# A band-attention and two-mixture kernel whose second mixture enters the list scheduler's plan, with scores and values of a half block in one piece

## The chip, the cores and the metric

The kernel runs on one core of a Trainium2 chip. Its time is the device time of one launch in microseconds (us). Engines are named as in the profile: PE (TensorE, matmuls and transposes; PEld its weight loads), DVE (VectorE), ACT (ScalarE), POOL (GpSimd) and SP, whose queue issues the loads and stores.

## The reference

Three stages on 2 x 768 tokens of 512 channels (8 heads of 64). The `scores` have a bias by distance, and all but the first `n_global` = 8 keys and the `n_local` = 96 latest are masked.

```python
scores = scale * np.matmul(q, k.transpose(0, 1, 3, 2)) + bias
a = np.exp(np.where(keep, scores, -1e9) - max); a = a / (sum(a) + 1e-9)
x = np.matmul(a, v)                              # heads side by side: B, S, 512
xk, xr = mu * x + (1.0 - mu) * x_prev            # mu_k and mu_r
k = np.maximum(xk @ w_k, 0.0);  v = k * k @ w_v  # 512 -> 1024 -> 512
x = v / (1.0 + np.exp(-(xr @ w_r)))
xn = (x - mu) / np.sqrt(var + 1e-06) * g_ln
out = x + np.maximum(xn @ w_ch1, 0.0) @ w_ch2    # 512 -> 2048 -> 512
```

The weights arrive as 64-bit floats. The accuracy wanted is that of 32-bit floats, so each matmul outside attention is done as three: high part by high part, high by low, low by high.

## The kernel before

**Tiles and stages.** Attention goes through 12 blocks of 128 tokens, each in two half blocks of 4 heads. A half block's chain is: scores on PE (`plan_scores`, L577) into two banks, DVE's minimum (L588), ACT's exponential (L594), PE's transposes (L612), ACT's copy of them (L428), PE's values (L626). Heads of 64 channels use the PE array by halves: scores two row halves, values two column halves, and other matmuls use the whole array. Scores and values are each planned as two operations of two heads. The first mixture has 6 groups of 256 tokens: POOL and DVE mix the input (L747 to L759), PE makes r (L796) and k (L830), ACT and DVE the square of the relu (L839, L840; POOL its low part, L845), PE v (L865 to L867, into the bank pair "b45"), DVE evicts v times r (L876), which frees the tanh's place that ACT needs for the next r (L801). The second mixture has 3 chunks of 512 tokens, each of 16 blocks f of 128 hidden channels: an up of 12 matmuls of 512 columns (L1017), ACT's relu (L1019), DVE's low part (L1020), then downs of 4 x 3 matmuls (L1032 to L1034).

**Weights.** A tile of 128 x 512 weights is loaded as 512 KB of integer pairs (the `stage` buffers and `tp`) and converted: a copy of the high words (ACT, POOL), three bit operations on DVE, the high part on ACT, the low part on DVE or POOL. There are 52 such tiles: 20 for the first mixture, and 32 for the second, of which 6 (EARLY) are in the plan and 26 (LATE) come behind it.

**What sets the order.** `Plan.play` (L134) is a list scheduler: operations with a cost on each engine that can do them, their inputs, the rooms (buffers) that they need and a due time. It takes, again and again, the operation that can start first, by due time where two can. Attention, the first mixture, the first 26 weights and the norms of chunk 0 are in that plan. The second mixture and the other weights are not: `mixture2` (L1041) is written behind it as loops (up f, then down f-1), and the later weights' conversions go, some steps at a time, in between. Their order on an engine's queue is left to the framework's own ordering, which draws conversions ahead into the first mixture's end. Engines run their queues in order.

Of the kernel before, what the change touches and what calls it, by code (L numbers as in the profile page):

```python
# [16 lines left out]
P = 128  # L17
# [16 lines left out]

CLOCK = {"PE": 8.0, "ACT": 8.0, "DVE": 9.5, "POOL": 8.0, "SP": 2.5}
# [4 lines left out]
TP_FROM = 20  # L40
LOW = {"POOL": 1440}


TM = (3, 9)
LNF = 12
# [46 lines left out]
def run(generator):  # L92
    for _ in generator:
        pass


# [8 lines left out]
class Plan:  # L105
# [11 lines left out]
    def op(self, engines, fn, reads=(), writes=(), rooms=(), due=0.0, behind=(), size=0):  # L117
# [13 lines left out]
        self.ops.append((engines, fn, deps, rooms, due, size))  # L131
        return i

    def play(self):  # L134
# [11 lines left out]
        dma = 0.0  # L146
        trace = []
        while open_:
            best = None
            for i in open_:  # L150
                engines, _, _, rooms, due, _ = self.ops[i]
# [21 lines left out]
            engines, fn, _, rooms, _, size = self.ops[i]  # L173
# [7 lines left out]
            end = t + engines[e]  # L181
            self.clock[e] = end
# [21 lines left out]
class Fast:  # L204
# [3 lines left out]
    def __init__(self, ctx, tc, a, w, ident):  # L208
# [4 lines left out]
        self.done = set()  # L213
        self.shut = set()
# [86 lines left out]

# [6 lines left out]

    def w_load(self, src):
        slot = self.slots.pop(0)  # L310
        raw = self.t([P, 512, 2], slot, I32, bufs={"stage": 2, "tp": 3}.get(slot, 1))
        self.nc.sync.dma_start(raw.rearrange("p n w -> p (n w)"), src.bitcast(I32))
        return slot, raw

    def w_split(self, slot, raw, hi, lo, scale):


        nc = self.nc
        low, high = raw[:, :, 0], raw[:, :, 1]
        y = self.t([P, 512], "cv", I32, bufs=2)  # L320
        yf = y.bitcast(F32)


        nc.scalar.activation(yf, high.bitcast(F32), AF.Copy, scale=2.0**-112)
        yield
        nc.vector.tensor_scalar(low, low, 29, None, ALU.logical_shift_right)
        yield
        nc.vector.scalar_tensor_tensor(low, high, -(1 << 31), low, ALU.bitwise_and, ALU.bitwise_or)
        yield
        nc.vector.scalar_tensor_tensor(y, y, 3, low, ALU.logical_shift_left, ALU.bitwise_or)  # L330
        if slot in ("stage", "tp", "nb"):
            self.slots.append(slot)
        yield
# [10 lines left out]
    def w_stream(self, items):  # L344


        self.items, self.raws = items, []
        self.bg = self.w_steps()
# [956 lines left out]
```

## Time and profile before

| what | value |
|---|---|
| time, median of 3 runs | 579.66 us (578.03 to 581.67) |
| profiled execution, own time | 578.45 us |
| its span, first to last instruction | 576.7 us |
| PE busy / DVE / ACT / POOL | 545.0 / 301.5 / 219.7 / 163.8 us |

Times in the rows further on count from the span's start. "Stretches" rows show how long each engine was busy in an interval, and the clock that was granted to PE, 1.00 being full (2.4 GHz). A wait's row names the engine and line that was waited for. The chain is the work that ended last, followed back from the end; a matmul that stands in it has its share of the elapsed time, which is shorter than the busy time of one matmul, since matmuls overlap. From 0 to 10 us the kernel loads and prepares, from 10 to about 152 it does attention, up to about 300 the rest of the first mixture, and up to 568 the second.

### The profile page before, as it was taken

How to read it: one execution, taken by the hardware profiler on the slowest of the kernel's cores; microseconds unless marked ns; L12 is line 12 of the kernel's file. 1: busy time of each engine (PE TensorE's matmuls, PEld its weight loads, DVE VectorE, ACT ScalarE, POOL GpSimd, SP SyncE). 2: the span in 40 equal slices, each digit the busy share in tenths (PEclk: the TensorE clock that was granted, in tenths of full speed). 3: DMA queues.
4: the chain of work that ended last, by engine and by line, in shares of the span. 5: the costliest groups of instructions: out<-in, count | busy, mean ns of one | idle time of the engine just before them, and what ended most of it. 6: DMA issues, size and time to landing. Idle time of an engine off the chain costs nothing.

```text
span 576.7 us, 8113 instructions
## 1 busy us (share of the span) xinstructions
PE 545.0 (95%) x3082; PEld 444.5 (77%) x3082; DVE 301.5 (52%) x651; ACT 219.7 (38%) x478; POOL 163.8 (28%) x202
## 2 busy tenths in 40 slices
PE   5979799999879999999799999999999999999995
PEld 3656577877679888989687888888888887888884
DVE  4877788886887364458959991243010133111012
ACT  3777787776753423235525650121011111101010
POOL 3466577644887535561310000010000000000000
PEclk9899999999999999999999999999999999999999
DMA  9899556332512010006424640001000001000002
GB/s 167 196 201 217 135 145 158 107 107 52 205 47 63 2 36 2 1 0 180 149 64 159 205 122 0 1 0 74 0 2 0 1 1 74 0 1 0 1 0 78
DMA packets 57307, 42.59 MB, mean 74 GB/s; under 512 B 49068, under 2 KB 49068, under 8 KB 57260
## 3 DMA queue, kind: packets, MB, share of 16 engines
q1 hardware_dynamic: 57084, 41.99, 27.3%
q8 instruction: 26, 0.43, 0.3%
q14 instruction: 21, 0.17, 0.1%
q0 software_dynamic: 32, 0.00, 0.0%
q10 hardware_dynamic: 144, 0.00, 0.0%
HBM read 38.84 MB, written 3.15 MB: 73 GB/s over the span
## 4 chain that ended last, share of the span: by engine, by line
PE 79%; DVE 9%; ACT 4%; DMA 3%; issue 1%; POOL 1%; SPq 1%; ACTq 0%; DVEq 0%; POOLq 0%
PE b L1017 23%; PE b L1032 8%; PE b L1034 8%; PE b L1033 8%; PE b L830 6%; PE b L796 6%; PE b L626 4%; PE b L577 3%; PE b L612 3%; PE b L865 2%; PE b L867 2%; PE b L866 2%; PE b L529 2%; ACT m L428 1%; DVE rt L752 1%
## 5 line engine op out<-in xcount | busy, mean ns | idle before, releaser
L1020 DVE SCALAR_TENSOR_TENSOR w<-b,w 128x512 fp32r<-128x512 f32 x48 | 33.1, 690 | 154.2 <-ACT w L1019 154.2
L1019 ACT ACTIVATE w<-b 128x512 fp32r<-128x512 f32 x48 | 28.7, 597 | 171.4 <-PE b L1017 171.3
L1032 PE MATMUL b<-w,w 128*128 128x512 f32 x192 | 75.6, 394 | 0.1
L1034 PE MATMUL b<-w,w 128*128 128x512 f32 x192 | 75.3, 392 | 0.0
L1033 PE MATMUL b<-w,w 128*128 128x512 f32 x192 | 75.0, 391 | 0.0
L986 POOL TENSOR_SCALAR st<-st 128x1 f32<-128x1 f32 x12 | 2.7, 225 | 174.2 <-DVE st L984 174.0
L830 PEld LDWEIGHTS b<-qA,w 128*128 128x128 f32 x384 | 48.1, 191 | 2.5 <-issue 1.2
L830 PE MATMUL b<-qA,w 128*128 128x256 f32 x384 | 48.9, 283 | 0.7 <-DVE rt L840 0.7
L594 ACT ACTIVATE tp<-tp,mn 128x232 f32<-128x232 f32 (+1 forms) x96 | 44.4, 466 | 5.6 <-DVE mn L588 5.4
L845 POOL TENSOR_TENSOR m<-rt,m 128x512 fp32r<-128x512 f32 x21 | 31.1, 1483 | 50.1 <-ACT m L841 50.1
L1032 PEld LDWEIGHTS b<-w,w 128*128 128x128 f32 x192 | 36.0, 188 | 9.0 <-DVE xg L1037 1.1
L1034 PEld LDWEIGHTS b<-w,w 128*128 128x128 f32 x192 | 36.0, 188 | 8.1 <-DVE w L1020 0.3
L1033 PEld LDWEIGHTS b<-w,w 128*128 128x128 f32 x192 | 36.1, 188 | 7.6
L752 DVE SCALAR_TENSOR_TENSOR rt<-xg,vec,rt 128x256 f32<-128x256 f32 x48 | 34.4, 762 | 10.9 <-POOL rt L747 10.9
L588 DVE CUSTOM_DVE_ANT_0 tp<-b,ln 128x232 f32<-128x232 f32 (+1 forms) x96 | 32.2, 372 | 14.2 <-PE b L577 13.9
L1017 PE MATMUL b<-kh,m 128*128 128x512 f32 x128 | 36.5, 394 | 0.0
L865 PE MATMUL b<-w,m 128*128 128x512 f32 x84 | 33.5, 399 | 3.0 <-ACT e L801 3.0
L700 POOL TENSOR_TENSOR w<-cv,w 128x512 fp32r<-128x512 f32 x20 | 27.8, 1392 | 23.0 <-ACT w L693 17.6
L867 PE MATMUL b<-w,m 128*128 128x512 f32 x84 | 33.2, 395 | 0.0
L866 PE MATMUL b<-w,m 128*128 128x512 f32 x84 | 33.1, 394 | 0.0
L612 PE MATMUL b<-ident,tp 128*116 128x128 f32 (+1 forms) x176 | 30.4, 284 | 1.7 <-ACT tp L594 1.5
L747 POOL TENSOR_SCALAR rt<-xg,vec 128x256 f32<-128x256 f32 x48 | 30.1, 641 | 1.7 <-DVE xg L666 0.8
(202 smaller groups left out, 1092.5 us busy)
## 6 DMA issues: line engine op xcount, KB each, us to landing
stage<-in_moe_w_ch_dram SPq DMA_DIRECT2D x22, 512.0 KB
tp<-in_moe_w_ch_dram SPq DMA_DIRECT2D x10, 512.0 KB
stage<-in_moe_w_k_dram SPq DMA_DIRECT2D x8, 512.0 KB
stage<-in_moe_w_v_dram SPq DMA_DIRECT2D x8, 512.0 KB
out_dram<-xg SPq DMA_DIRECT2D x12, 256.0 KB
m<-in_v_dram SPq DMA_DIRECT2D x10, 192.0 KB
qA<-in_q_dram SPq DMA_DIRECT2D x7, 256.0 KB
stage<-in_moe_w_r_dram SPq DMA_DIRECT2D x2, 512.0 KB
```

Of the source, the lines that this page charges most:

```text
L594: nc.scalar.activation(t, t, AF.Exp, bias=mn.tile[:, k : k + 1], scale=-1.0, accum_out=sm.tile[:, h : h + 1])
L612: nc.tensor.transpose(b.tile[0:w, c, k * P : (k + 1) * P], tp.tile[:, k, c * w : (c + 1) * w], self.ident)
L752: nc.vector.scalar_tensor_tensor(y.tile[:, u], z, v, y.tile[:, u], ALU.mult, ALU.add)
L796: nc.tensor.matmul(b.tile, *seq[s], start=s == 0, stop=s == 11)
L830: nc.tensor.matmul(o, l, r, start=s == 0, stop=s == 11)
L865: nc.tensor.matmul(ps, hi, wh, start=f == 0, stop=False)
L866: nc.tensor.matmul(ps, hi, wl, start=False, stop=False)
L867: nc.tensor.matmul(ps, lo, wh, start=False, stop=f == 7)
L1017: nc.tensor.matmul(ps, l, r, start=s == 0, stop=s == 11)
L1032: nc.tensor.matmul(ps, hi[:, sl], wh, start=f == 0, stop=False)
L1033: nc.tensor.matmul(ps, hi[:, sl], wl, start=False, stop=False)
L1034: nc.tensor.matmul(ps, lo[:, sl], wh, start=False, stop=f == 15)
```

## The change

The second mixture is in the plan: `plan_second`, `plan_up` and `plan_down` replace `mixture2`, `m2_up` and `m2_down`, and all 52 weight tiles are converted by `plan_weight`. A late weight's low part may go to DVE or POOL, and the copy of its high words to ACT or POOL. Scores of a half block (now L472) and its values (L522) are one operation each. The planner adds 95 ns to a PE operation that uses the array in another way than the one before (`mode`), and some of its costs differ. The norms of the next chunk stand at blocks 8 to 11 of a chunk instead of 12 to 15, and the small operations that test the tokens outside the band (`last`) are planned too. No arithmetic of the outputs is changed.

```diff
-                if j + 1 < NTOK // 512 and f >= LNF:
-                    self.flush()
-                    run(self.m2_norm(j + 1, f - LNF))
...
-TP_FROM = 20
-LOW = {"POOL": 1440}
-TM = (3, 9)
-LNF = 12
+LATE0, LATE1 = -10.0, 3.3
+TP_FROM, TP_TO = 24, 44
+LOW, LATE_LOW = {"POOL": 1440}, {"DVE": 715, "POOL": 1500}
+LNF = 8
...
+    SWITCH = 95.0
...
             end = t + engines[e]
+            if e == "PE" and way != mode:
+                end += self.SWITCH
+                mode = way
...
-        for j in range(2):
-            c = 2 * hf + j
-            s = hf if n == 0 else 0
-            def scores(e, j=j, c=c):
-                for k in (2 * j, 2 * j + 1):
...
-            p.op({"PE": 40 + 1.6 * w}, scores, reads, [("S", i, j)], banks + [self.Q, self.K], due + 0.5 * j)
+        def scores(e):
+            for k in range(4):
+                r, c = slice((k % 2) * D, (k % 2 + 1) * D), 2 * hf + k // 2
+                nc.tensor.matmul(S(k), self.qT(n)[r, c], self.kT()[r, c, c0:c1], start=True, stop=True)
...
+        p.op({"PE": 3.4 * w}, scores, reads, [("S", i)], banks + [self.Q, self.K], due, mode="rows")
...
-            op = p.op({"PE": 218 * m}, values, [("pT", i), ("v", n % 3)], [("O", n, hf, j)], [self.O[n], self.V[n], y], due + 9 + j)
+        op = p.op({"PE": 436 * m}, values, [("pT", i), ("v", n % 3)], [("O", n, hf)], [self.O[n], self.V[n], y], due + 9, mode="columns")
...
-        p.op({"ACT": 670, "POOL": 1100}, lambda e: self.copy(e, yf(), high().bitcast(F32), 2.0**-112), [R], [C], [raw, cv, w], due - 2, behind=behind)
-        p.op({"DVE": 460}, lambda e: nc.vector.tensor_scalar(low(), low(), 29, None, ALU.logical_shift_right), [R], [(R, 1)], [raw], due - 2)
+        p.op({"ACT": 670, "POOL": 850}, lambda e: self.copy(e, yf(), high().bitcast(F32), 2.0**-112), [R], [C], [raw, cv] + wr, due - 2, behind=behind)
+        p.op({"DVE": 500}, lambda e: nc.vector.tensor_scalar(low(), low(), 29, None, ALU.logical_shift_right), [R], [(R, 1)], [raw], due - 2)
...
-        p.op({"DVE": 745} if scale is not None else LOW, rest, [C, HI], [key], [cv, w], due)
-        return w
+        p.op({"DVE": 745} if scale is not None else (LOW if j < 20 else LATE_LOW), rest, [C, HI], [key], [cv] + wr, due)
...
+            self.plan_second(j, x, at[NG])
+            p.op({"DVE": 3000}, lambda e: last(), due=at[NG] + 150)
             self.trace = p.play()
-            last()
-        self.deep = 2
-        self.slots = ["stage", "stage", "tp"]
-        self.w_stream([getattr(self, f"{k}_item")(*r) for k, *r in LATE])
...
+    def plan_second(self, j0, x, start):
+        nc, a, p = self.nc, self.a, self.plan
+        for i, (k, *r) in enumerate(LATE):
+            due = start + LATE0 + LATE1 * i
+            if k == "w1":
+                self.plan_w1(j0 + i, *r, due, [x[-1]] if r[0] == 2 else [])
...
+        for j in range(n):
+            acc = [self.bank_room(3), Room("b45", 1, self.banks), None, self.bank_room(6)]
+            for f in range(16):
+                at = start + 88 * j + 5.5 * f
+                self.plan_up(j, f, at)
+                self.plan_down(j, f, at + 4, acc)
+                if j + 1 < n and LNF <= f < LNF + 4:
+                    self.plan_norm(j + 1, f - LNF, at, self.loads if j == 0 else [])
...
+    def plan_up(self, j, f, due):
...
+        self.up = [p.op({"PE": 2750}, products, reads, [U], [b] + self.xn_rooms[j], due, behind=self.up)]
+        p.op({"ACT": 600}, lambda e: nc.scalar.activation(u.tile[:, 0], b.tile, AF.Relu), [U], [(U, 0)], [b, u], due + 3)
...
+    def plan_down(self, j, f, due, acc):
...
+            p.op({"PE": 688}, products, [(U, 0), (U, 1), ("w2", f)], [("acc", j, tb)], [u, room], due + 0.1 * tb)
```

Where lines move: scores L577 to L472, transposes L612 to L507, values L626 to L522, k L830 to L747, r L796 to L713, v L865 to L782, its eviction L876 to L793, up L1017 to L915, down L1032 to L938, the relu's low part L1020 to L923; on DVE the conversion's L326, L328, L330, L337, L339 to L591, L592, L593, L599, L601.

The instruction order of PE in attention, where one half block's values and the next one's scores stood in two parts, before:

```order
L626 MATMUL b_290_1567<-m_287_1538,m_216_1143 64x128 x4
L612 MATMUL b_292_1597<-ident,tp_1445 116x128 x8
L577 MATMUL b_295_1612<-kh_139,qA_126 128x232
L577 MATMUL b_296_1613<-kh_139,qA_126 128x232
L529 MATMUL b_297_1617<-ident,kh_139 128x128 x4
L577 MATMUL b_295_1612<-kh_139,qA_126 128x232
L577 MATMUL b_296_1613<-kh_139,qA_126 128x232
```

and at a place of the new order:

```order
L507 MATMUL b_294_1609<-ident,tp_1499 116x128 x2
L472 MATMUL b_295_1613<-kh_139,qA_126 128x232
L472 MATMUL b_296_1614<-kh_139,qA_126 128x232
L472 MATMUL b_295_1613<-kh_139,qA_126 128x232
L472 MATMUL b_296_1614<-kh_139,qA_126 128x232
L426 MATMUL b_298_1624<-ident,kh_139 128x128 x4
L507 MATMUL b_294_1609<-ident,tp_1499 116x128 x6
```

Of 24 half blocks, 9 had their scores split and 5 their values; now none has: four score rows stand together, and the values are "L522 x8".

POOL's order behind attention (rt and qA belong to the first mixture's input, w to a converted weight, m to the square's low part), before:

```order
L759 TENSOR_TENSOR kh_1877<-rt_1876,kh_1877 128x512
L759 TENSOR_TENSOR kh_1877<-rt_1891,kh_1877 128x512
L747 TENSOR_SCALAR rt_1939<-xg_735,vec_121 128x256 x2
L747 TENSOR_SCALAR rt_1961<-xg_735,vec_121 128x256 x2
L759 TENSOR_TENSOR qA_1940<-rt_1939,qA_1940 128x512
L759 TENSOR_TENSOR qA_1940<-rt_1961,qA_1940 128x512
L845 TENSOR_TENSOR m_363_2015<-rt_2014,m_363_2015 128x512
L845 TENSOR_TENSOR m_366_2033<-rt_2032,m_366_2033 128x512
```

and now, where a weight's copy (L329) has come in ahead of qA's two low parts:

```order
L601 TENSOR_TENSOR w_340_1883<-cv_1882,w_340_1883 128x512
L601 TENSOR_TENSOR w_343_1907<-cv_1906,w_343_1907 128x512
L664 TENSOR_SCALAR rt_1964<-xg_782,vec_121 128x256 x2
L664 TENSOR_SCALAR rt_1981<-xg_782,vec_121 128x256 x2
L329 TENSOR_SCALAR cv_2002<-stage_1944 128x512
L676 TENSOR_TENSOR qA_1965<-rt_1964,qA_1965 128x512
L676 TENSOR_TENSOR qA_1965<-rt_1981,qA_1965 128x512
L664 TENSOR_SCALAR rt_2052<-xg_1348,vec_121 128x256 x2
```

DVE's order at the end of the first mixture, where the eviction of a v tile (L876, L793) frees the tanh's place, before:

```order
L337 SCALAR_TENSOR_TENSOR qA_3148<-cv_3166,vec_121,qA_3148 128x512
L337 SCALAR_TENSOR_TENSOR qA_3148<-cv_3211,vec_121,qA_3148 128x512
L326 TENSOR_SCALAR stage_3218<-stage_3218 128x512
L330 SCALAR_TENSOR_TENSOR cv_3243<-cv_3243,stage_3176 128x512
L328 SCALAR_TENSOR_TENSOR stage_3218<-stage_3218 128x512
L326 TENSOR_SCALAR tp_3221<-tp_3221 128x512
L330 SCALAR_TENSOR_TENSOR cv_3257<-cv_3257,stage_3218 128x512
L339 TENSOR_TENSOR w_185_978<-cv_3243,w_185_978 128x512
L328 SCALAR_TENSOR_TENSOR tp_3221<-tp_3221 128x512
L876 SCALAR_TENSOR_TENSOR xg_2998<-e_2579,b_456_2900 128x512
L876 SCALAR_TENSOR_TENSOR xg_2998<-e_2622,b_456_2900 128x512
```

and now:

```order
L591 TENSOR_SCALAR stage_2978<-stage_2978 128x512
L599 SCALAR_TENSOR_TENSOR qA_3030<-cv_3029,vec_121,qA_3030 128x512
L757 SCALAR_TENSOR_TENSOR rt_3052<-b_456_2857,rt_3052 128x512
L601 TENSOR_TENSOR w_476_3022<-cv_3021,w_476_3022 128x512
L793 SCALAR_TENSOR_TENSOR xg_3073<-e_2589,b_463_2935 128x512
L793 SCALAR_TENSOR_TENSOR xg_3073<-e_2629,b_463_2935 128x512
L757 SCALAR_TENSOR_TENSOR rt_3076<-b_472_2986,rt_3076 128x512
```

Nine conversion operations stood ahead of the evictions in the rows shown; now two and a k square (L757) do. Over the rest of DVE's queue, 56 conversion operations stood behind the first L1020; 69 stand behind the first L923, as far as the fourteenth block of chunk 0.

## Rows read from the trace of the kernel before

**Rows 1.** The page's part 1: busy us of each engine (share) x instructions

```profile
PE 545.0 (95%) x3082; PEld 444.5 (77%) x3082; DVE 301.5 (52%) x651; ACT 219.7 (38%) x478; POOL 163.8 (28%) x202
```

**Rows 2.** Stretches: from:to, us, each engine's busy us, granted clock, DMA share, GB/s

```profile
10.00:152.00 142.00, 128.66 (x1051) 96.46 (x1047) 111.53 (x321) 106.73 (x291) 79.07 (x92) 0.99 0.65 158
...
183.00:282.00 99.00, 97.65 (x600) 86.89 (x600) 55.36 (x89) 36.18 (x62) 44.67 (x52) 1.00 0.14 43
...
300.00:345.00 45.00, 45.00 (x197) 36.58 (x196) 40.93 (x85) 25.64 (x42) 0.00 (x0) 1.00 0.52 164
```

**Rows 3.** The chain that ended last: start us, us, work

```profile
320.31 2.75 PE b L1017 x12
```

**Rows 4.** PE's waits, 10 to 152: waiting <- waited for: us, times, longest

```profile
PE b L626 <- ACT m L428: 4.1, 6, 1.2
```

**Rows 5.** PE's waits, 152 to 300 us

```profile
PE b L830 <- DVE rt L840: 3.7, 2, 3.0
PE b L865 <- ACT e L801: 3.0, 1, 3.0
PE b L993 <- DVE ln L989: 0.6, 1, 0.6
```

**Rows 6.** The chain, 166 to 171 us

```profile
166.57 2.72 POOL qA L759
...
169.31 0.61 ACT rt L839
...
169.94 0.69 DVE rt L840
```

**Rows 7.** The chain, 285 to 293 us

```profile
285.82 0.61 DVE xg L876
...
286.45 0.61 ACT e L801
...
287.17 0.47 PE b L865
...
288.28 2.56 PE b L796 x6
...
291.75 1.39 PE b L796 x6
```

**Rows 8.** Two short stretches behind the stops, columns as in rows 2

```profile
173.00:175.00 2.00, 2.00 (x12) 2.00 (x11) 2.00 (x2) 0.72 (x1) 1.90 (x3) 0.50 0.76 203
289.00:291.00 2.00, 2.00 (x6) 1.59 (x5) 1.96 (x3) 0.00 (x0) 1.32 (x1) 0.50 0.58 166
```

**Rows 9.** The chain in attention: whole and half pieces

```profile
35.75 1.05 PE b L577 x8
...
44.60 0.66 PE b L577 x4
...
83.43 0.98 PE b L577 x8
...
111.79 1.02 PE b L626 x16
...
114.95 0.66 PE b L626 x8
...
116.19 0.59 PE b L626 x8
```

**Rows 10.** PE's instructions, timeline: start us, us, engine, line, operation

```profile
281.69 0.39 PE L867 MATMUL b<-w,m 128*128 128x512 f32 x1
```

**Rows 11.** Groups, whole span: out<-in xcount | busy, mean ns | idle before

```profile
L691 DVE SCALAR_TENSOR_TENSOR stage<-stage 128x512 int32<-128x512 int32 x22 | 19.3, 877 | 0.3
```

**Rows 12.** Groups of DVE from 300 to 345 us

```profile
L328 DVE SCALAR_TENSOR_TENSOR stage<-stage 128x512 int32<-128x512 int32 x10 | 6.8, 686 | 0.0
L1020 DVE SCALAR_TENSOR_TENSOR w<-b,w 128x512 fp32r<-128x512 f32 x8 | 5.5, 685 | 0.0
L326 DVE TENSOR_SCALAR stage<-stage 128x512 int32<-128x512 int32 x10 | 4.3, 426 | 2.8 <-DMA stage<-in_moe_w_ch_dram 2.8
```

More of the change, by code (lines that the diff above doesn't have):

```diff
@@ L619, in plan_weighted, with values @@
             self.O[n] = self.bank_room(6)
-        for j in range(2):
-            def values(e, j=j):
+        def values(e):
+            for j in range(2):
                 for c in range(m):
@@ new lines, in plan_up, with products @@
+    def plan_up(self, j, f, due):
+        nc, p = self.nc, self.plan
+        b = self.bank_room(f % 3)
+        u = self.u = self.room(f"w{16 + f % 2}", 1, [P, 2, 512], F32R)
+        o = (f % 4) * P
+        def products(e):
+            xh, _, xl = self.xn[j]
+            w = [tuple(y[:, o : o + P] for y in self.w1[f // 4, c]()) for c in range(4)]
+            seq = [(w[c][0], xh[:, c, :]) for c in range(4)] + [(w[c][1], xh[:, c, :]) for c in range(4)]
+            seq += [(w[c][0], xl[c]) for c in range(4)]
+            for s, (l, r) in enumerate(seq):
+                nc.tensor.matmul(b.tile, l, r, start=s == 0, stop=s == 11)
+        U = ("up", j, f)
+        reads = [("norm", j, s) for s in range(4)] + [("w1", f // 4, c) for c in range(4)]
+        self.up = [p.op({"PE": 2750}, products, reads, [U], [b] + self.xn_rooms[j], due, behind=self.up)]
+        p.op({"ACT": 600}, lambda e: nc.scalar.activation(u.tile[:, 0], b.tile, AF.Relu), [U], [(U, 0)], [b, u], due + 3)
+        p.op(
+            {"DVE": 690},
+            lambda e: nc.vector.scalar_tensor_tensor(u.tile[:, 1], b.tile, 0.0, u.tile[:, 0].bitcast(F32), ALU.max, ALU.subtract),
+            [U, (U, 0)], [(U, 1)], [b, u], due + 3,
+        )
@@ new lines, in plan_down, with products @@
+    def plan_down(self, j, f, due, acc):
+        nc, p = self.nc, self.plan
+        u, U = self.u, ("up", j, f)
+        place = lambda tb: acc[1].tile[:, tb - 1] if tb in (1, 2) else acc[tb].tile
+        for tb in range(4):
+            room = acc[1 if tb in (1, 2) else tb]
+            def products(e, tb=tb):
+                hi, lo = (u.tile[:, i, tb * P : (tb + 1) * P] for i in range(2))
+                wh, wl = self.W[f]
+                ps = place(tb)
+                nc.tensor.matmul(ps, hi, wh, start=f == 0, stop=False)
+                nc.tensor.matmul(ps, hi, wl, start=False, stop=False)
+                nc.tensor.matmul(ps, lo, wh, start=False, stop=f == 15)
+            p.op({"PE": 688}, products, [(U, 0), (U, 1), ("w2", f)], [("acc", j, tb)], [u, room], due + 0.1 * tb)
+            if f < 15:
+                continue
+            r = (4 * j + tb) * P
+            x = lambda tb=tb: self.x1[2 * j + tb // 2][:, (tb % 2) * 512 : (tb % 2 + 1) * 512]
+            p.op({"DVE": 690}, lambda e, tb=tb, x=x: nc.vector.tensor_tensor(x(), place(tb), x(), ALU.add), [("acc", j, tb)], [("x1", 2 * j + tb // 2, tb % 2)], [room], due + 1)
+            p.op({"SP": 60}, lambda e, r=r, x=x: nc.sync.dma_start(self.a["out"].rearrange("b s d -> (b s) d")[r : r + P, :], x()), [("x1", 2 * j + tb // 2, tb % 2)], [("out", r)], (), due + 1)
```

266 lines of the change are left out of this document (75 added, 191 removed).

## Prediction

> **What bounds the kernel now.** I read the page's busy times first. TensorE (PE) works 545.0 of the span's 576.7 us; DVE, the next, 301.5 [rows 1]. So a part of the change counts only if it takes work or idle time from PE, or gives it new idle time. The table of stretches says where the idle time is [rows 2]: 13.3 us (142.00 - 128.66) during attention, from 10 to 152 us; after that PE has 97.65 of 99.00 us, and from 300 to 345, at the second mixture's start, 45.00 of 45.00. The second mixture, whose code the change rewrites most, has no idle time of PE to give back. Twelve of its matmuls take 2.75 us [rows 3], as they will afterwards.
>
> The waits tell what the idle time is. In attention no wait rules: the largest group is 4.1 us in six waits of value products for ScalarE's copy of the transposed probabilities [rows 4]. Behind attention there are three groups, 3.7, 3.0 and 0.6 us [rows 5], and two of these waits are single ones of 3.0 us. The chain names both. The first: at 166.57 POOL begins a low part of 2.72 us into the mixed input qA, ScalarE's relu of a k tile follows at 169.31 and DVE's square at 169.94, and only then has the next k tile a place [rows 6]. The second: at 285.82 DVE evicts a value tile, at 286.45 ScalarE can write the tanh whose place this frees, at 287.17 PE goes on [rows 7].
>
> Both cost more than their length. After the first the granted clock was 0.50 of full, the lower level of 1.2 GHz, and so it was after the second [rows 8]. Six 512-column matmuls took 2.56 us at 288.28 and 1.39 us at 291.75 [rows 7]: 1.17 us lost on these six, and with the three before them, 0.3 to 0.5 us more. I count 1.5 us for each such stretch.
>
> **The change part by part.** *Joined pieces.* Before, 9 of 24 half blocks have their scores in two parts with other work between, and 5 have their values so; afterwards none (counted in the instruction order, of which the change's section shows a place). A whole score piece took 0.98 to 1.05 us and a half 0.66; a whole value piece 1.02 and a half 0.59 to 0.66 [rows 9]. A split score piece therefore costs 2 x 0.66 - 1.02 = 0.30 us more, a split value piece 1.25 - 1.02 = 0.23. That gives 9 x 0.30 + 5 x 0.23 = 3.9 us. Half pieces that meet another of their shape save less, so I take 3.6; bounds 2 (only scores, at 0.22) and 4.6.
>
> The rest of attention is moved about, and every weight's conversion shifts by some places. The transposes-copy-values chain of a half block keeps its length, and PE has the same other work to lay beside it, but 3.6 us less of it. I take 0 for the waits and bound it by 3 us each way: 3 us more is most of the saved work turned into waiting, 3 us less is most of the 4.1 us group.
>
> *Hand-over behind attention.* The waits here were 3.0, 0.7 and 0.6 us [rows 5]. POOL still makes the two low parts of kh and the two of qA in the new order, but with one copy of a weight before those of qA; by then PE has the value products of the first group and the k products whose input is there. I follow PE's new order with the measured durations: it runs out before the same k tile for about 2.5 us, once more for 0.6, and a value tile later on has only four short norm transposes before it to cover its predecessor's two evictions and a tanh, 3 x 0.61 [rows 7], which leaves about 1.2. That sum is 4.3, as before: 0, bounds 2.5 each way. Whether a stop of 2.5 us still lowers the clock no row tells: the two of 3.0 us did, while attention's waits for L428, of at most 1.2 us, leave its mean granted clock at 0.99 [rows 2, 4]. I take half of the 1.5 us: -0.75.
>
> *The late stop, at 284.* This is the term that the planner changes most. Before, the conversions of the late weights stood in DVE's queue by no plan: nine conversion operations precede the two evictions in the rows shown, and PE's last product of that value tile was done at 282.1 [rows 10], 3.7 us before its first eviction, which still stood in that queue, began [rows 7]. In the new order the evictions (L793) come behind one k square and one conversion. I follow it: v done, 0.7 to 1.2 us to the end of the first eviction, 0.6 ScalarE's tanh, 0.1 for signals: 1.4 to 1.9 us, and up to 2.4 with one more conversion of 0.69 in the way [rows 12]. Against the measured stop of about 3.1 that saves 1.2, and since a stop of 1.9 is nearer to those that left the clock alone, 1.4 of the slow stretch too: -2.6, bounds 0 (DVE is late by as much as now) and -4.5 (no stop).
>
> *Second mixture.* Same matmuls, in pairs of two ups and two downs instead of one of each. PE has nothing to give here; it can lose. Cover of the rest: between an up and its downs stand ScalarE's relu (0.6) and DVE's low part (0.69), and the other up of 2.75 us hides both [rows 3, 6, 12]. Behind the first relu 69 conversion operations remain on DVE, where there were 56. At 0.43 us for the first step and 0.69 for the others [rows 12], about 0.65 on average, these are 13 x 0.65 = 8.5 us more DVE time beside PE. Before, DVE worked 40.93 of the 45 us from 300 to 345 [rows 2], and PE lost nothing; the new order spreads its conversions as far as the fourteenth of the 16 blocks of the first chunk, about 75 us, so there is room. I take 0, bounds 0 and +6. The norms of the next chunk begin four blocks earlier, and the flag computation on DVE (L70 to L88), which stood among the second mixture's first conversions, moves into attention; both are short beside that.
>
> **Sum.** -3.6 + 0 + 0 - 0.75 - 2.6 + 0 = -6.95, against the profiled execution's 578.45 us: 571.5 us. That execution lies 1.2 us under the median of the three runs, 579.66, so by the median the change is about 1.4%. One per cent, 5.8 us, is what a measurement of this kernel can tell from no change.
>
> **Rivals.**
> *All stops close.* The planner now sees conversions, evictions and products in one list; if it places them as the chip runs them, the first stop ends under 1.5 us and both slow stretches go: a further 1.5 to 2.5 at the hand-over, 0.75 of clock, 1.9 at the late stop and 1 to 2 in attention. That gives 564 to 566 us. Against it: my walk of the new order finds the v tile's eviction directly ahead of what needs its place.
>
> *The saved work turns into waiting.* DVE worked 111.53 and ScalarE 106.73 of attention's 142 us [rows 2]; if a half block's chain of score, minimum, exponential, transpose, copy and value sets attention's pace, shorter PE pieces only wait longer, and a joined score piece must wait for both its banks where a half waited for less. Then -3.6 becomes 0 to -1, and with one of the two later stops unchanged the time is 575 to 578. For it: the 4.1 us group [rows 4]. Against it: the bulk of attention shows PE at nine tenths of its time [rows 2], so work, not waiting, was most of it. The same time results if the plan does not do what it says at 284, that is if late conversions still stand before the evictions.
>
> *Slower: DVE falls behind in the second mixture.* The relu's low part (L923) and the conversions share DVE's queue. In attention, with POOL busy 79.07 of 142 us, a two-operand conversion step took 877 ns on average; from 300 to 345, with POOL at 0.00, 686 [rows 2, 11, 12]. In the new plan POOL makes more of the copies, some of them within the second mixture. If DVE's steps there take 877 rather than 686, 69 x 0.19 = 13 us are added to the 8.5 us more that it has to do. Where the low part comes later than the 2.75 us of the other up allow, PE waits in each of some 12 blocks; 1 us apiece and two more stretches at half clock are 15 us: 586. It decides from about 0.9 us of wait per block, and PE must wait there at all, which before it never did. The Trainium skill (GPSIMD Engine Reference, section Specifications) says that POOL shares its interfaces to SBUF with VectorE and contends with DVE instructions that have two SBUF inputs. The two durations above agree with it. By that rule the price is paid only while POOL works, and a few copies of about 1 us each would lengthen only the steps that they overlap, which makes this rival small.
>
> **How the numbers follow.** The forecast, with its terms' bounds taken together (568 to 574), has 0.50; all stops close 0.13; the saved work turns into waiting 0.25; DVE falls behind 0.12, of which 0.08 goes beyond 585.5. The predicted time is that of the first, 571.5. Below 573.9 (faster by over 1%) lie the second case and nearly all of the first: 0.61. Between lie the rest, 0.31; slower 0.08. The range reaches from 563 (all stops close) to 580 (waiting in full, with a little loss to DVE) and leaves out about 0.15, most of it above.
>
> **What would show it.** Joined pieces: the score line with 24 pieces of near 1 us and PE's busy time of attention about 3.6 us lower. Late stop: ScalarE's tanh named under 2 us as PE's releaser, and no half clock after it. Hand-over: the square of relu (now L757) as releaser with about 3 us. Second mixture: PE full in every stretch; waits of the down products for L923 would mean the third rival. Wrong would be: PE's busy time in attention unchanged, a stop of 3 us with a half clock behind it near 285, or PE under 99% between 300 and 430 us.

## The result, and the profile after

After the change the kernel takes 570.23 us (median of 4 runs, 569.59 to 572.95); the kernel before took 578.85 beside it (577.40 to 581.67). The ratio is 0.9852, with a 95% interval of 0.9808 to 0.9896. A second measurement, made with the experiments below, gave 569.98 against 578.21, ratio 0.9859 [0.9843, 0.9876]. The prediction was 571.5 us, in a range of 563 to 580.

The profiled execution of the first measurement is its slowest, 572.95 us, because a stretch at half clock came near its start, from about 12 to 22 us (the granted clock of 12 to 22 is 0.52, in the table below; attention's last value product starts at 147.65 us in it and at 144.63 in the second). The second measurement's profiled execution, 569.81 us with a span of 568.0, is close to the median. Both are used. First the page's busy times after the change, answering [rows 1]:

```profile
PE 540.9 (95%) x3082; PEld 445.2 (78%) x3082; DVE 307.4 (54%) x649; ACT 213.9 (37%) x471; POOL 167.3 (29%) x211
```

Then the stretches, answering [rows 2], with columns as there:

```profile
10.00:152.00 142.00, 131.02 (x1066) 102.28 (x1065) 109.37 (x333) 107.12 (x294) 79.74 (x92) 0.96 0.64 152
152.00:183.00 31.00, 28.38 (x182) 25.30 (x181) 30.17 (x37) 12.90 (x21) 22.33 (x22) 1.00 0.27 85
183.00:282.00 99.00, 95.37 (x589) 84.72 (x588) 60.31 (x90) 37.21 (x63) 49.92 (x54) 1.00 0.14 43
282.00:300.00 18.00, 18.00 (x79) 14.63 (x78) 10.21 (x17) 4.81 (x8) 0.87 (x2) 1.00 0.28 87
300.00:345.00 45.00, 44.98 (x200) 36.63 (x200) 36.49 (x65) 17.63 (x28) 6.44 (x10) 1.00 0.41 129
345.00:430.00 85.00, 85.00 (x383) 69.59 (x382) 36.15 (x66) 17.98 (x32) 4.31 (x12) 1.00 0.11 38
...
12.00:22.00 10.00, 9.05 (x44) 6.52 (x44) 7.24 (x45) 5.03 (x19) 2.91 (x4) 0.52 0.99 219
```

PE is full from 282 us on. Its waits from 150 to 310 us, answering [rows 5], of the first and of the second profile after:

```profile
PE b L747 <- DVE rt L757: 3.7, 3, 2.5
PE b L713 <- ACT e L718: 1.4, 1, 1.4
PE b L782 <- DVE xg L793: 1.0, 1, 1.0
```

```profile
PE b L747 <- DVE rt L757: 3.3, 2, 2.5
```

(the other two are the same in it). The hand-over's stop of 2.5 us is still there, and the late stop is 1.4 us. The chain of the first profile there, answering [rows 7]:

```profile
277.97 0.24 PE b L784
...
278.24 0.70 DVE xg L793
...
278.96 0.61 ACT e L718
...
279.61 1.66 PE b L713 x6
...
281.96 1.39 PE b L713 x6
```

The eviction begins with the end of the product that it needs, and the six matmuls behind the stop take 1.66 us, not 2.56: no half clock. **Where the 8.7 us between the spans went** (576.7 before, 568.0 in the second profile after) is read from two marks, attention's last value product and the last down matmul. Before:

```profile
150.96 1.09 PE L626 MATMUL b<-m,m 116*64 116x128 f32 x16
...
569.83 0.40 PE L1034 MATMUL b<-w,w 128*128 128x512 f32 x1
```

and in the second profile after:

```profile
144.63 1.09 PE L522 MATMUL b<-m,m 116*64 116x128 f32 x16 [0.86 <-ACT m L325]
...
559.95 0.39 PE L940 MATMUL b<-w,w 128*128 128x512 f32 x1
```

Attention ends 6.3 us earlier (150.96 - 144.63); from there to the last down it is 418.9 before and 415.3 after, another 3.5; behind the last down it is 6.9 before and 8.05 after, 1.2 given back. In the first profile after, where the clock stays full behind the hand-over and in the second it does not, attention's end to the last down takes 414.6 us (147.65 to 562.21), 4.3 less than before.

### The profile page after: what moved, and what is told of

The parts are those of the page before. It is cut to its first block, busy times and chain, and to the rows that moved or that the text cites. A ratio compares the mean times of both kernels' runs of the same rounds, so it can differ in the third digit from the quotient of the medians.

```text
span 571.1 us, 8093 instructions
## 1 busy us (share of the span) xinstructions
PE 540.9 (95%) x3082; PEld 445.2 (78%) x3082; DVE 307.4 (54%) x649; ACT 213.9 (37%) x471; POOL 167.3 (29%) x211
## 4 chain that ended last, share of the span: by engine, by line
PE 83%; DVE 10%; ACT 3%; POOL 1%; issue 1%; POOLq 0%; ACTq 0%; DVEq 0%
PE b L915 23%; PE b L747 9%; PE b L938 8%; PE b L940 8%; PE b L939 8%; PE b L713 6%; PE b L472 3%; PE b L522 3%; PE b L782 3%; PE b L784 3%; PE b L783 3%; PE b L507 3%; PE b L426 2%; DVE rt L669 2%; DVE stage L592 1%; DVE stage L591 1%
## 5 line engine op out<-in xcount | busy, mean ns | idle before, releaser
L923 DVE SCALAR_TENSOR_TENSOR w<-b,w 128x512 fp32r<-128x512 f32 x48 | 33.2, 692 | 159.8 <-ACT w L920 159.8
L938 PE MATMUL b<-w,w 128*128 128x512 f32 x192 | 75.3, 392 | 0.0
L747 PEld LDWEIGHTS b<-qA,w 128*128 128x128 f32 x384 | 48.0, 190 | 3.5 <-DVE rt L757 1.8
L747 PE MATMUL b<-qA,w 128*128 128x256 f32 x384 | 48.8, 283 | 1.4 <-DVE rt L757 1.3
L938 PEld LDWEIGHTS b<-w,w 128*128 128x128 f32 x192 | 36.0, 188 | 8.2 <-DVE xg L793 0.4
L762 POOL TENSOR_TENSOR m<-rt,m 128x512 fp32r<-128x512 f32 x21 | 28.3, 1351 | 40.2 <-ACT m L758 40.2
L593 DVE SCALAR_TENSOR_TENSOR cv<-cv,stage 128x512 int32<-128x512 int32 x44 | 34.7, 790 | 7.4 <-ACT cv L325 4.9
L592 DVE SCALAR_TENSOR_TENSOR stage<-stage 128x512 int32<-128x512 int32 x44 | 37.0, 843 | 0.7
L915 PE MATMUL b<-kh,m 128*128 128x512 f32 x128 | 36.2, 394 | 0.0
L669 DVE SCALAR_TENSOR_TENSOR rt<-xg,vec,rt 128x256 f32<-128x256 f32 x48 | 31.0, 695 | 9.3 <-POOL rt L664 9.3
L601 POOL TENSOR_TENSOR w<-cv,w 128x512 fp32r<-128x512 f32 x20 | 27.4, 1370 | 25.4 <-ACT w L594 25.2
L782 PE MATMUL b<-w,m 128*128 128x512 f32 x84 | 33.5, 398 | 1.0 <-DVE xg L793 1.0
L329 POOL TENSOR_SCALAR cv<-stage 128x512 f32<-128x512 f32 x22 | 17.4, 792 | 54.1 <-DMA stage<-in_moe_w_ch_dram 22.9
```

Source lines behind the costliest of these rows:

```text
L592: p.op({"DVE": 760}, lambda e: nc.vector.scalar_tensor_tensor(low(), high(), -(1 << 31), low(), ALU.bitwise_and, ALU.bitwise_or), [R, (R, ...
L593: p.op({"DVE": 760}, lambda e: nc.vector.scalar_tensor_tensor(y(), y(), 3, low(), ALU.logical_shift_left, ALU.bitwise_or), [(R, 2)], [C], ...
L669: nc.vector.scalar_tensor_tensor(y.tile[:, u], z, v, y.tile[:, u], ALU.mult, ALU.add)
L747: nc.tensor.matmul(o, l, r, start=s == 0, stop=s == 11)
L782: nc.tensor.matmul(ps, hi, wh, start=f == 0, stop=False)
L915: nc.tensor.matmul(b.tile, l, r, start=s == 0, stop=s == 11)
```

## The experiments

Each kernel is compared with runs of the kernel before on the same chip, at 578.1 to 578.7 us.

**Joined pieces alone.** The kernel before, with only the scores and the values of a half block made one operation each:

```diff
-            p.op({"PE": 40 + 1.6 * w}, scores, reads, [("S", i, j)], banks + [self.Q, self.K], due + 0.5 * j)
+        p.op({"PE": 3.4 * w}, scores, reads, [("S", i)], banks + [self.Q, self.K], due)
...
-            op = p.op({"PE": 218 * m}, values, [("pT", i), ("v", n % 3)], [("O", n, hf, j)], [self.O[n], self.V[n], y], due + 9 + j)
+        op = p.op({"PE": 436 * m}, values, [("pT", i), ("v", n % 3)], [("O", n, hf)], [self.O[n], self.V[n], y], due + 9)
```

> The kernel before, with the scores and the values of a half block planned and issued in one piece each and nothing else changed (no cost of a mode change, second mixture not in the plan). If the joined pieces are worth the 3.6 us of TensorE work that the prediction counted, the ratio to the kernel before is about 0.994 (575 us of 579), TensorE's busy time from 10 to 152 us is lower by 3 to 4 us at the same work, and the two stops at the hand-over and at the end of the first mixture stay near 3 us each. If the saved work only turns into waiting, the ratio is 0.998 to 1.002 and the value products' waits for L428 grow from 4.1 to about 7 us.

Measured: 578.28 against 578.08 us, ratio 1.0017 [0.9986, 1.0048]. No gain. The work was saved all the same. By the groups of attention, scores, values and transposes together kept PE busy for 83.1 us before, 77.6 here and 77.3 in the second profile after the whole change; some 1.5 us of the difference belong to a half-clock stretch near 15 us that the profile of before has and this one has not. Part of what the kernel lost is in its waits from 150 to 310 us, 9.8 us where before had 8.4:

```profile
PE b L864 <- ACT e L800: 4.2, 2, 3.1
PE b L864 <- DVE xg L875: 3.0, 1, 3.0
PE b L829 <- DVE rt L839: 1.9, 2, 1.5
PE b L829 <- POOL kh L758: 0.7, 1, 0.7
```

The stop of 3.0 us for an eviction of v (L875) is new. DVE's queue ahead of it (start us, us, what):

```profile
175.18 1.33 DVE L689 TENSOR_SCALAR stage<-stage 128x512 int32<-128x512 int32 x1
176.54 1.40 DVE L326 TENSOR_SCALAR tp<-tp 128x512 int32<-128x512 int32 x1
177.98 0.69 DVE L328 SCALAR_TENSOR_TENSOR tp<-tp 128x512 int32<-128x512 int32 x1
178.59 1.28 DVE L875 SCALAR_TENSOR_TENSOR xg<-lo,b 128x512 f32<-128x512 f32 x2
```

L326 and L328 convert a weight of the second mixture. They stand there by no plan: the framework drew them ahead of the eviction as soon as a `tp` buffer was free. In attention, too, PE waits longer: from 10 to 150 us its waits sum to 13.4 us here and 11.3 before, though not where it was expected (the value products' waits for L428 are 3.8 us). So 2.1 us up to 150 us and 1.4 behind it, 3.5 of the 3.6 us that the pieces were to save, came back as waiting. What the many small waits in attention hang on was not tested.

**The same, without that buffer for late weights.** The kernel above, with late weights loaded into the two `stage` buffers only:

```diff
-        self.slots = ["stage", "stage", "tp"]
+        self.slots = ["stage", "stage"]
```

> The kernel of the first experiment (the kernel before with joined pieces), in which the late weights' loads may use only the two stage buffers and not the one of tp. In the first experiment's trace PE stopped 3.1 us at 180, a stop that the kernel before did not have: two conversion steps of a late weight in tp, 2.1 us, that the framework had drawn ahead, stood in DVE's queue between the k square and the two evictions. Without tp these two steps are gone from there and the evictions follow directly. If they turned the saved work into waiting, the stop falls to about 1 us and the time from 578.3 to about 576, ratio 0.996. If something else takes their place, PE's waits from 150 to 310 us still sum to about 10 us and the time stays at 578 or rises, since the late weights now come with one buffer less.

Measured: 574.78 against 578.35 us, ratio 0.9940 [0.9917, 0.9963], some 3.5 us better than joined pieces alone. The stop of 3.0 us is 0.8, that for the tanh 1.0:

```profile
PE b L829 <- DVE rt L839: 2.5, 3, 1.5
PE b L864 <- ACT cv L324: 1.8, 1, 1.8
PE b L864 <- ACT e L800: 1.0, 1, 1.0
...
PE b L864 <- DVE xg L875: 0.8, 1, 0.8
PE b L1033 <- DVE w L1019: 0.8, 1, 0.8
```

So the conversions in DVE's queue did make the 3.0 us stop and, it seems, much of the stop for the tanh. But most of that waiting only moved: with two buffers in place of three PE has small new waits (L864 for the copy at L324, and L1033 in the second mixture, where it works 43.69 of the 45 us from 300 to 345), and its waits from 10 to 310 us sum to 21.8 us, where joined pieces alone had 23.2 and the kernel before 19.7. Its executions lie between 573.75 and 579.41 us; the profiled one is the longest, with its granted clock at 0.83 from 10 to 30 us. At a mean clock of 0.996 to 0.999 they took 573.75 to 574.31 us, joined pieces alone 574.88 to 575.61 at 0.998: at equal clock about 1.2 of the 3.5 us remain. That the rest is clock saved by the missing stops is likely but not shown.

**Joined pieces with the planner's price of 95 ns.** The kernel of the first experiment, with the charge for a PE operation that uses the array in another way than the one before:

```diff
+            if e == "PE" and way != mode:
+                end += 95.0
+                mode = way
```

> The kernel before with joined scores and values, as in the first experiment, and with the planner's 95 ns for a change of TensorE's mode; the second mixture stays outside the plan. Without that price the joined pieces gained nothing here. If the planner's picture of TensorE's time is what turns the saved work into time, attention gets shorter by 3 to 4 us (last value product at about 147 us of the span where no stretch of half clock falls into it) and the time is 574 to 576, ratio 0.993 to 0.995, with the late stop near 3 us as before. If the gain needs the second mixture's plan, because conversions that the framework draws ahead stop DVE and with it PE elsewhere, the time is 577 to 579 and PE's waits from 150 to 310 us sum to 8 us or more.

Measured: 577.96 against 578.21 us, ratio 0.9996 [0.9968, 1.0024]: no gain either. The price does not make the difference while the late weights are outside the plan.

**The whole change, with the pieces split again.** The reverse of the first diff, in the kernel after.

> The changed kernel with scores and values in two pieces each, as before; the second mixture stays in the plan. Now 14 of 24 half blocks have their scores in two parts. By the prices of the prediction (0.30 us a split score, 0.23 a split value) that is 14 x 0.30 + 3 x 0.23 = 4.9 us more: about 575 us, ratio 0.993, with the late stop still at 1.4 us as in the changed kernel. If joining was worth nothing, 570 to 571 us, ratio 0.985.

Measured: 575.88 against 578.08 us, ratio 0.9973 [0.9952, 0.9994], 5.7 us over the kernel after. Fourteen scores and three values are split in this order, which by the prediction's prices is 14 x 0.30 + 3 x 0.23 = 4.9 us. The late stop is as short as after the change:

```profile
PE b L714 <- ACT e L719: 1.4, 1, 1.4
```

so the pieces and the late stop are separate terms. PE's waits from 10 to 310 us sum to 16.8 us here, and to 16.8 and 17.4 in the two profiles after: what was lost is work and not waiting, and within this plan the pieces bring their full price.

**The whole change, without the 95 ns.**

```diff
-    SWITCH = 95.0
+    SWITCH = 0.0
```

> The changed kernel with the planner's price for a change of TensorE's mode at 0 instead of 95 ns; only the order changes. The joined pieces stay, and the number of mode changes in the order is about the same. If the joined pieces alone make the gain in attention, the time stays within 1 us of 570.2 and the last value product at 145 to 148.5 us of the span. If the planner's better picture of TensorE's time is needed to turn the saved work into time (joining alone in the kernel before gained nothing), the last value product comes 2 to 3 us later and the time is 572 to 573.

Measured: 576.11 against 578.66 us, ratio 0.9963 [0.9941, 0.9985]: 6 us lost by one number. It is not the number of changes of the array's use: with score rows, value rows and all other matmuls told apart, PE's order in the trace has 88 runs of one use here and 91 in the kernel after. It is another order, in which PE's waits from 10 to 310 us sum to 21.9 us in place of 16.8: in attention PE waits once for the mixing of an input,

```profile
PE b L557 <- DVE qA L433: 3.8, 1, 3.8
```

the granted clock is at its lower level from 65 us on for some 7 us, and the last value product comes at 152.28, against 144.63.

**The late stop: an eviction that is repeated.** In the kernel after, the first eviction of the fifth group's v is done five times in a row (L793, the same result each time); the order is unchanged.

```diff
+            def evict(e, tb=tb, ev=ev):
+                for _ in range(5 if (g, tb) == (4, 0) else 1):
+                    nc.vector.scalar_tensor_tensor(x1.tile[:, tb * 512 : (tb + 1) * 512], ev(), 1.0, b.tile[:, tb], ALU.add, ALU.mult)
...
+                {"DVE": 690}, evict,
```

> The changed kernel, in which DVE makes the first eviction of the fifth group's value tile five times instead of once; the planner knows nothing of it, so every engine's order is the same. It puts four operations of about 0.61 us, 2.4 us in all, into DVE's queue at the late stop and nowhere else. If PE's late stop hangs on DVE's queue, it grows from 1.4 to about 3.8 us, the time by 2.4 us (572.6), and by 1.5 us more (574.1) if a stop of that length brings a stretch of half clock. If the stop hangs on something else, it stays under 2 us and the time at 570.

Measured: 575.65 against 578.66 us, ratio 0.9946 [0.9925, 0.9966], 5.4 us over the kernel after. The stop grew by 2.9 us, four steps of 0.72 (0.61 each was expected):

```profile
PE b L713 <- ACT e L718: 4.3, 1, 4.3
```

and the clock fell behind it: the chain's `L713 x6` took 2.93 us at 281.16 where it took 1.66 after. The stretches:

```profile
281.00:283.00 2.00, 1.84 (x4) 1.49 (x5) 2.00 (x5) 1.30 (x3) 0.52 (x1) 0.50 0.03 8
283.00:285.00 2.00, 2.00 (x6) 1.58 (x5) 2.00 (x3) 0.65 (x1) 0.76 (x1) 0.50 0.00 0
```

This stop thus hangs on what DVE does before ACT's tanh, step by step. Of the 5.4 us, 2.9 are the longer stop, and the other 2.5 fit the stretch at half clock behind it.

**Late weights' due times 30 us earlier** (`LATE0` -40 for -10), meant to crowd DVE's queue at the late stop.

> The changed kernel with the late weights due 30 us earlier in the plan (LATE0 -40 instead of -10). Four conversion steps then stand directly ahead of the first eviction of the value tile whose places PE waits for, where there were two operations with a k square between, and two more ahead of the second. If DVE's queue makes the late stop, as the prediction says, it grows from 1.4 us by about 2 to 2.5 us to nearly 4, a stretch of half clock (1.5 us) follows it, and the time is about 574, ratio 0.992. If the stop comes from what the value tile itself needs (the tanh's path), it stays near 1.4 us and the time at 570, ratio 0.985.

Measured: 571.45 against 578.08 us, ratio 0.9888 [0.9843, 0.9932]. The planner moved PE's work as well; the place of the late stop went to the second mixture's first up (L915, 1.5 us for L757), and the hand-over stayed at 2.5. The run does not test what it was meant to.

**The hand-over.** Two ways to keep conversions out of DVE's queue there. First, the planner reckons 1000 ns for the first conversion step of weights 18 to 23:

```diff
-        p.op({"DVE": 500}, lambda e: nc.vector.tensor_scalar(low(), low(), 29, None, ALU.logical_shift_right), [R], [(R, 1)], [raw], due - 2)
+        p.op({"DVE": 1000 if 18 <= j < 24 else 500}, lambda e: nc.vector.tensor_scalar(low(), low(), 29, None, ALU.logical_shift_right), [R], [(R, 1)], [raw], due - 2)
```

> The changed kernel, in which the planner takes 1000 instead of 500 ns for DVE's first conversion step of weights 18 to 23; only the order changes. In the changed kernel's trace PE stops 2.5 us at the hand-over because a step of a weight's conversion, at 1.5 us instead of 0.43 while POOL makes qA's low parts, stands in DVE's queue ahead of the k tile's square. Here two of the three conversion steps there go behind the square. If the queue's order is the cause, the stop falls from 2.5 to about 1 us and the time to about 568.8, ratio about 0.983. If POOL's low part of qA (the prediction's own reading) is the cause, the stop stays at 2.3 to 2.6 us and the time at 570.

Measured: 568.43 against 578.08 us, ratio 0.9835 [0.9794, 0.9875]. Second, only weight 20 waits with that step until the k products are issued (`behind=[self.k_op] if 20 <= j < 21 else ()`, at the same operation):

> The changed kernel in which only the first of the early weights' first conversion step must wait for the k products then last planned; 72 conversion steps then stand behind the first relu instead of 69. If DVE's queue makes the hand-over's stop, it falls from 2.5 us to about 1 without the loss that the 30 moved steps of the overloaded version brought to the second chunk's norms: 568 to 569 us, ratio 0.983. If the moved steps are still too much for the second mixture, PE waits for norms or low parts there and the time is 570 or more.

Measured: 568.63 against 578.21 us, ratio 0.9834 [0.9818, 0.9850]; its four executions took 567.46 to 569.04 where those of the kernel after, on the same chip, took 569.67 to 570.81. Both are the best that was run, by 1.4 us or so. The waits from 150 to 310 us of 0.3 us and more in the first, and the hand-over's stop in the second:

```profile
PE b L747 <- DVE rt L757: 1.5, 2, 1.2
PE b L713 <- ACT e L718: 1.4, 1, 1.4
PE b L975 <- DVE ln L971: 1.1, 1, 1.1
```

```profile
PE b L747 <- DVE rt L757: 1.9, 1, 1.9
```

In the kernel after, the square (L757) that ends the stop stands behind three conversion steps in DVE's queue, and two of these are slow. DVE's timeline:

```profile
165.61 1.79 DVE L599 SCALAR_TENSOR_TENSOR m<-cv,vec,m 128x512 fp32r<-128x512 f32 x1
167.32 1.51 DVE L591 TENSOR_SCALAR stage<-stage 128x512 int32<-128x512 int32 x1
168.86 0.85 DVE L592 SCALAR_TENSOR_TENSOR stage<-stage 128x512 int32<-128x512 int32 x1
169.63 0.68 DVE L757 SCALAR_TENSOR_TENSOR rt<-b,rt 128x512 f32<-128x512 f32 x1
```

and POOL's beside it:

```profile
165.38 3.17 POOL L676 TENSOR_TENSOR qA<-rt,qA 128x512 fp32r<-128x512 f32 x2
```

ACT's relu for this square had ended at 167.50 (166.89 + 0.60), so 2.1 us of the stop are DVE's queue. The queue costs so much because its steps are slow there: at the 0.75 and 0.42 us that L599 and L591 take elsewhere, it would have been done as the relu ended. In the second kernel the stop fell to 1.9 us and not to 1, as expected, since two other conversion steps, of 1.70 and 1.57 us beside POOL, still stand ahead of the square.

**Four weights held back.** The same `behind` for weights 20 to 23 puts 99 conversion steps behind the second mixture's first relu, where the kernel after has 69 (`20 <= j < 24`).

> The changed kernel, in which the first conversion step of the early weights must wait for the k products then last planned, so that their conversions leave the hand-over and 99 conversion steps, 30 more, stand behind the first relu on DVE. Reading by DVE's queue: no conversion stands ahead of the k square at the hand-over, and the stop there falls from 2.5 us to about 1. For the second mixture the rival of the prediction says that a DVE overloaded like this (30 x 0.65 = 19.5 us more) makes the relu's low parts late and PE wait, by 10 us or more: over 578 us. If DVE has the room that its 36 of 45 us in the changed kernel's trace suggest, PE stays nearly full from 300 us on and the time is 568 to 573.

Measured: 573.28 against 578.66 us, ratio 0.9921 [0.9892, 0.9950], some 3 us over the kernel after. No conversion stands ahead of the square at the hand-over now, DVE idles 2.2 us until ACT's relu comes, and of the stop 0.4 us are left:

```profile
PE b L747 <- DVE rt L757: 0.4, 1, 0.4
```

That is all that POOL's low part and the relu cost by themselves. But 5 us of waits appear where the second chunk is normed. PE's waits from 310 to 440 us:

```profile
PE b L975 <- DVE ln L971: 4.9, 3, 2.6
PE b L939 <- DVE w L601: 0.3, 1, 0.3
```

and the stretches, the second at half clock behind the stop:

```profile
345.00:430.00 85.00, 79.82 (x349) 64.42 (x348) 39.25 (x73) 18.80 (x32) 7.10 (x13) 0.96 0.16 50
372.00:376.00 4.00, 1.37 (x6) 1.25 (x6) 3.77 (x8) 1.42 (x3) 1.08 (x2) 0.58 0.00 0
```

No down waits for the relu's low part (L923), although DVE has nearly half as many steps again.

**No POOL for late weights.** Copies on ACT and low parts on DVE alone:

```diff
-LOW, LATE_LOW = {"POOL": 1440}, {"DVE": 715, "POOL": 1500}
+LOW, LATE_LOW = {"POOL": 1440}, {"DVE": 715}
...
-        p.op({"ACT": 670, "POOL": 850}, lambda e: self.copy(e, yf(), high().bitcast(F32), 2.0**-112), [R], [C], [raw, cv] + wr, due - 2, behind=behind)
+        p.op({"ACT": 670, "POOL": 850} if j < 26 else {"ACT": 670}, lambda e: self.copy(e, yf(), high().bitcast(F32), 2.0**-112), [R], [C], [raw, cv] + wr, due - 2, behind=behind)
```

> The changed kernel with the 26 late weights' copies planned for ScalarE alone and their low parts for DVE alone, so that POOL has no work on them. If POOL's work slows DVE's two-operand steps there (877 against 686 ns in the kernel before), the mean of these steps from 300 to 345 us falls by some per cent, but since PE has no stop there the time stays at 569 to 571.5 us, ratio 0.985. If DVE was at its limit in the second mixture, the time moves by 2 us or more, either way: down by less contention, or up by ScalarE's longer queue.

Measured: 571.34 against 578.66 us, ratio 0.9864 [0.9824, 0.9904], within about 1 us of the kernel after. From 300 to 345 us DVE's steps L593 and L599 (into m) took 704 and 834 ns after, and here:

```profile
L593 DVE SCALAR_TENSOR_TENSOR cv<-cv,stage 128x512 int32<-128x512 int32 x10 | 6.7, 681 | 0.2
...
L599 DVE SCALAR_TENSOR_TENSOR m<-cv,vec,m 128x512 fp32r<-128x512 f32 x4 | 2.9, 747 | 1.0 <-ACT m L594 1.0
```

POOL does lengthen DVE's steps there, a little, and nothing waits for it.

**The kernel after once more**, for the result and its second profile above.

> The changed kernel once more, for a second profile. In its first profile a stretch of half clock lay from 12.4 to 22.6 us and the last two stores took over 1.2 us each to issue; that execution was 2.4 us longer than the median of the others. If both belong to that one execution, this profile's span is about 568 us and its last value product comes at 145 to 146 us; if they belong to the kernel, both are here again. The three later stops (2.5, 1.4 and 1.0 us) are the same in either case, and the time is 569.5 to 571.

## Why the prediction was right, point by point

The time, 570.2 against 571.5, comes mostly from the terms that were forecast: from the end of attention to the last down the kernel gained 3.5 us where the sum had 3.35. In attention it gained 6.3 where the sum had 3.6, and 1.2 of that was given back at the end, which the sum did not have. So the total is near partly because two misses of opposite sign cancel.

*Joined pieces, -3.6: the size was right.* In the second profile after, scores take 24.5 us in place of 26.6 and values 24.5 in place of 26.1, 3.7 us less; transposes, of which nothing was said, take 28.3 in place of 30.4. About 1.5 of these 5.8 us are the early half-clock stretch that stands in the profile of before, which leaves 4.3; with 0.7 us less waiting this is near the 4.8 us by which attention is shorter at equal clock (6.3 - 1.5). Splitting the pieces again cost 5.7 us for a price of 4.9. But the prediction took it for granted that PE's saved time would be time saved. In the kernel before it is not: joined alone, the pieces gave nothing. The rival "the saved work turns into waiting" has that kernel's time, but not by attention's chain, whose waits for L428 did not grow; the one long stop that is new is DVE's queue. What saved the forecast is the order of the whole change, with the late conversions in the plan and the 95 ns in its costs; without the 95 ns the same plan gave 576 us. In the sum the pieces and the plan stood as independent terms; they are not, and that this order lets the pieces count was not worked out beforehand: to that extent the forecast was lucky.

*Waits in attention, 0 with 3 either way.* From 10 us to the end of attention PE's waits sum to 10.7 and 11.7 us in the two profiles after, against 12.4 before. Right in size, but it holds only for this order: without the 95 ns the same code has a stop of 3.8 us there and loses 6 us. I had read the price as a detail; the largest sensitivity in the study hangs on it.

*Hand-over, stops of 2.5, 0.6 and 1.2: right in size, not in cause.* They are 2.5, 0.8 to 1.2 in sum, and 1.0. The prediction explained the first, as in [rows 6], by POOL's low part, ACT's relu and DVE's square. In the kernel after the relu was done 2.1 us before the square began, and the conversions stood in between; two kernels that only move these took the stop down to 1.2 and 1.9 us, and a third to 0.4, while POOL still makes the low parts. POOL enters through DVE's durations.

*Half the half clock, -0.75: one profile for it and one against.* Behind the same stop of 2.5 us the granted clock is full in the first profile after and falls in the second. The second's stretch:

```profile
168.00:172.00 4.00, 4.00 (x20) 3.71 (x20) 3.32 (x5) 1.25 (x2) 1.29 (x1) 0.57 0.40 131
```

A stop of 2.5 us is thus one that brings it in some executions. Two profiles do not say in how many, and the timed executions of the kernel after, nearly all at a mean clock of 0.992 to 0.994, look more like the second (0.994) than like the first hand-over kernel, whose stop is 1.2 us (0.995 to 0.998 in three of four executions): the term may have been nearer 0. In the second profile the 3.5 us gained behind attention hold nothing of it; by the prediction's own price of a stretch, the late stop brought about 3 of them.

*Late stop, 1.4 to 1.9 us and full clock, -2.6: right.* It is 1.4 us, the low end, since DVE was idle when the product came and no conversion was in its way; the six matmuls behind it run at full clock. So the stop is 1.6 us shorter, where the sum had 1.2 (and took 3.1 us for a stop that [rows 5] has at 3.0). DVE's row in the first profile after, with its idle time in brackets:

```profile
278.24 1.28 DVE L793 SCALAR_TENSOR_TENSOR xg<-e,b 128x512 f32<-128x512 f32 x2 [1.03 <-PE b L784]
```

With the eviction repeated, the stop and the half clock came back and cost 5.4 us.

*Second mixture, 0: right.* PE has 44.98 of 45 us and all of the next 85. The rival of DVE falling behind does not occur here, and when 30 more conversion steps were pushed there it came by another way than forecast: not through the relu's low parts but through the norms of the next chunk, which stand among conversions in DVE's queue (L971 ready late), with 4.9 us of waits and a half clock. The Trainium skill (GPSIMD Engine Reference, section Specifications) has POOL contend with DVE instructions that have two SBUF inputs or run in a 2-port perf mode. The measured steps agree: where POOL works on late weights a two-input step took 0.02 to 0.09 us longer, against the 0.19 that the rival took.

*What was left out: the end.* Before, the last downs waited 0.5 us for a bank and the evictions were spread; now they run through, and three evictions end behind the last matmul. The ends of the chain before and in the second profile after:

```profile
570.27 0.69 DVE xg L1037
```

```profile
559.70 1.89 DVE xg L947 x3
```

The last eviction so ends 1.6 us after the last down began, not 1.1, and the rest of the 1.2 us lies in the stores behind it. Without this the time would have been about 569.

*What the comparison of single profiles hides.* The sum started from an execution of before at 578.45 us with three half-clock stretches, and counted two. At a mean granted clock of 0.993 the executions of before that were timed took 574.15 and 575.02 us, and those of the kernel after, at 0.992 to 0.994, 569.59 to 570.81. So about 4 to 5 us of the gain are work and waits at equal clock, and the other 4 that the kernel before usually has a lower clock (0.987 to 0.990 in most executions). The prediction had 4.8 and 2.15. How much of that is the early stretch near 15 us, which both kernels have in some executions, stays open; no run changed the start of the program.

## What to carry to other kernels

Work taken from the busiest engine is a gain only where the other engines' queues let the next work start earlier: look for what stands in an in-order queue ahead of the step that frees a buffer, and count an operation there at its own duration in stop. Work that is optional in time, such as converting later weights, belongs into the same plan as the evictions, with due times; but a plan is only as good as its costs, and one number, the 95 ns, was worth 6 us here. When a stop's releaser is the last of a chain, check when its own input was ready; if that was long before, the queue is the cause and not the chain.

## What the runs showed of the hardware that was not expected

- DVE's steps grow beside POOL more than the average of [rows 11] tells. While POOL ran two-input operations, a conversion step of one input and a constant (L591) took 1.51 us and one of two inputs (L599) 1.79; alone they took 0.42 and 0.75.
- One kernel, one stop, two outcomes: the stop of 2.5 us at the hand-over left the clock full in one execution and at 0.57 for 4 us in another. The executions of joined pieces alone spread with their mean clock: 574.88 to 575.61 us at 0.998, 578.16 to 578.34 at 0.992, 578.93 and 579.67 at 0.989, 581.72 and 582.19 at 0.982 and 0.984. Which stops make that spread was not looked at execution by execution, since there is one profile of them.
